# Retention attention and two feed-forward layers in one kernel: the state summed in PSUM with scaled tables, and a written order for everything up to the fourteenth product

## The chip, the cores and the metric

One core of one Trainium2 chip. The metric is the device time of one execution of the whole program in microseconds, the median of three runs; beside it stands one execution taken by the hardware profiler, whose span runs from its first to its last instruction.

## The reference

Attention with a decaying state over 2 batches of 8 heads, 768 positions and 64 features, then two feed-forward layers over the 1536 tokens of 512 features, all in float32:

```python
for t in range(S):
    state = gamma[None, :, None, None] * state + np.einsum('bhd,bhe->bhde', k[:, :, t], v[:, :, t])
    y[:, :, t] = scale * np.einsum('bhd,bhde->bhe', q[:, :, t], state)
...
rms = np.sqrt(np.mean(x * x, axis=-1, keepdims=True) + 1e-06)
xn = x / rms * rms_g
g = xn @ w_gate
silu = g * (1.0 / (1.0 + np.exp(-g)))
x = silu * (xn @ w_val) @ w_out          # d_ff 1536
...
h = x @ w_in                             # d_ff 2048
out = np.maximum(0.01 * h, h) @ w_out
```

`gamma` has one value for each head, the same at every position. The weights come as float64 bits and are converted on the chip.

## The kernel before

**Attention.** The 1536 tokens are 12 chunks of 128, six for each batch. A chunk holds 4 pairs of heads; a pair's two heads lie on partitions 0 to 63 and 64 to 127. For a chunk c the steps are, by the names of the functions: `scores` (eight matmuls on halves of the rows, k against q, into one of two score buffers), `decay_scores` (DVE multiplies by the mask of decays, tile `a`), `decay_k` (k by a table over the positions, tile `kd`; on DVE for chunks 0 and 1, on POOL from 2), `outer` (kd against v for a pair of heads at once, so that a 128 by 128 product `u` is made of which the two 64 by 64 blocks on the diagonal are used), `decay_state` (POOL: the old state by its decay, `tmp`), `update` (DVE: the two blocks of `u` plus `tmp`, one instruction for each half of the partitions, into one of two `state` tiles), `decay_q` (POOL, `qs`), `before` (the state against qs into `y`), `heads` (v against `a`, added into the same `y`), `squares` (ScalarE: y squared, and y times the gain in four instructions, `xg`), and `sums_of_squares` (DVE, one reduction). y alternates between two PSUM banks.

Two chunks together are then normalised: `total` (PE sums over the partitions), `mean` (DVE), `rsqrt` (POOL), `spread` (PE, back over the partitions), `scaled` (DVE: xg times it), `high` (ScalarE) and `rest` (DVE), which split x into a high and a low part, `xh` and `xl`, for three blocks of 512 tokens.

**Weights.** Each block of 512 KB is fetched by SyncE's queue into one of three raw buffers and converted: `prepare` (two ScalarE instructions), `smaller`, `shifted`, `sign`, `add` (DVE), `high_part` (ScalarE), `low_part` (DVE). For most weights sums and differences of two are made too (keys with an s).

**Layers.** A product (`whole`, L460) is twelve matmuls of 128 by 128 by 512: eight with the high part of x and four with the low. `gated`, `times` and `leaky` take it out of PSUM; `down` adds into four banks (L488). `quad` makes the products of two features with two blocks in seven half products (L662). `plan` lists all steps; `run` does one and lets `convert` do a number of weight steps behind it.

**Order.** Every engine works through its queue in the order in which the instructions were issued. In the attention the loop over the chunks is written out (lines 816 to 867): the tail of one chunk stands among the next chunk's steps, the total of a pair three chunks after its first. The loads of chunks 0 to 4 are issued ahead of the loop, the others four chunks ahead in it; some weight steps stand behind each chunk (`CONVERT`). The last pairs' norms are put between the first products (`late`). The first fourteen steps of the plan are the twelve products of features 0 and 1 with three blocks and two `down`:

```python
for i, (keys, b, step) in enumerate(steps[:FIXED]):
    for do in late.get(i, []):
        do()
    run(i, keys, b, step, RATE0)
```

Of the kernel before, what the change touches and what calls it, by code (L numbers as in the profile page):

```python
# [37 lines left out]
BLOCKS = [512, 512, 512]  # L38


@with_exitstack
def chain_kernel(ctx: ExitStack, tc: tile.TileContext, qk_t, kv, w1, w2, mask, qdec, kdec, sdec, rms_g, ident, out):
# [24 lines left out]
    at = attn_pools.enter_context(tc.tile_pool(name="at", bufs=2))  # L67
    at1 = attn_pools.enter_context(tc.tile_pool(name="at1", bufs=1))
# [4 lines left out]
    kdec_sb = const.tile([P, 2 * NPAIR, 1], F32, name="kdec_sb")  # L73
    sdec_sb = const.tile([P, NPAIR, 1], F32, name="sdec_sb")
# [4 lines left out]
    state = [const.tile([P, NPAIR, P], F32, name=f"state{i}") for i in range(2)]  # L79
# [18 lines left out]
    def load_chunk(c):  # L98
        if c < EARLY:
            a, b = (units.tile([P, 2, 512], F32, tag="u", name=f"{n}{c}") for n in ("qkT", "kv"))  # L100
        elif c < EARLY + len(SPARE):
            t = xp.tile([P, 4, 512], F32, tag=SPARE[c - EARLY], name=f"qkv{c}")
            a, b = t[:, :2], t[:, 2:]
        else:
            a, b = (at.tile([P, 2, 512], F32, tag=n, name=f"{n}{c}") for n in ("qkT", "kv"))
        nc.sync.dma_start(out=a, in_=qk_t[c])
        ch[c] = {"qkT": a, "kv": b}
        if c == 1:
            nc.sync.dma_start(out=qdec_sb, in_=qdec)
        if 2 < c < 6:  # L110
            fetch()
        nc.sync.dma_start(out=b, in_=kv[c])
        if c == 0:
            for j in range(2):
                nc.sync.dma_start(out=mask_sb[:, j], in_=mask[:, j])
# [9 lines left out]
    def decay_k(c):  # L125
        if not last(c):
            s = ch[c]
            s["kd"] = at1.tile([P, 2 * NPAIR, D], F32, tag="kd", name=f"kd{c}")
            e = nc.vector if c < 2 else nc.gpsimd
            e.tensor_tensor(  # L130
                out=s["kd"],
                in0=s["kv"][:, 0, :].rearrange("p (h d) -> p h d", d=D),
                in1=kdec_sb.to_broadcast([P, 2 * NPAIR, D]),
                op=ALU.mult,
            )

    def decay_q(c):
        if c % CPB:
            s = ch[c]
            s["qs"] = at1.tile([P, NPAIR, CH], F32, tag="qs", name=f"qs{c}")  # L140
            nc.gpsimd.tensor_tensor(out=s["qs"], in0=by_pair(s["qkT"][:, 0, :]), in1=qdec_sb, op=ALU.mult)

    def decay_state(c):
        if c % CPB and not last(c):
            s = ch[c]
            s["tmp"] = by_pair(scratch(f"tmp{c}"))
            nc.gpsimd.tensor_tensor(
                out=s["tmp"], in0=state[(c + 1) % 2], in1=sdec_sb.to_broadcast([P, NPAIR, P]), op=ALU.mult
            )
# [16 lines left out]

    def outer(c):
        if not last(c):
            s = ch[c]
            s["u"] = u = acc_bank(2, f"u{c}")  # L170
            kd = s["kd"].rearrange("p h d -> p (h d)")
# [4 lines left out]
    def update(c, j):  # L176
        if not last(c):
            s = ch[c]
            r = slice(j * D, (j + 1) * D)
            new, u = state[c % 2][r, :, r], by_pair(s["u"])[r, :, r]  # L180
            if c % CPB:
                nc.vector.tensor_tensor(out=new, in0=u, in1=s["tmp"][r, :, r], op=ALU.add)
            else:
                nc.vector.tensor_copy(new, u)

    def before(c):
        s = ch[c]
        s["y"] = y = acc_bank(c % 2, f"y{c}")
        for a in range(NPAIR if c % CPB else 0):
            nc.tensor.matmul(  # L190
                out=y[:, a * CH:(a + 1) * CH],
                lhsT=state[(c + 1) % 2][:, a, :],
                rhs=s["qs"][:, a, :],
                start=(a == 0),
                stop=False,
                skip_group_check=True,
            )

    def heads(c):
        s = ch[c]  # L200
        for a in range(NPAIR):
# [11 lines left out]
    def squares(c):  # L213
        s = ch[c]
        b = block_of(c)
        y = s["y"]
        s["sq"] = sq = scratch(f"sq{c}")
        nc.scalar.activation(out=sq, in_=y, func=AF.Square)
# [3 lines left out]
        for a in range(NPAIR):  # L222
            nc.scalar.activation(
                out=xg[b][:, a, o:o + CH], in_=y[:, a * CH:(a + 1) * CH], func=AF.Copy, scale=g_sb[:, a, :]
            )

    def sums_of_squares(c):
        s = ch[c]
        s["ss"] = sm.tile([P, CH], F32, tag="ss", name=f"ss{c}")
        nc.vector.tensor_reduce(out=s["ss"], in_=s["sq"].rearrange("p (a t) -> p t a", a=NPAIR), op=ALU.add, axis=AX.X)  # L230

    def total(cs):
        nrm[cs] = {"bank": acc_bank(3, f"norm{cs[0]}")}
        for i, c in enumerate(cs):
            o = 2 * CH + i
            nc.tensor.matmul(out=nrm[cs]["bank"][:, o:o + 1], lhsT=ch.pop(c)["ss"], rhs=ones, start=True, stop=True)

    def mean(cs):
# [4 lines left out]
        nc.vector.tensor_scalar(w["a"], w["bank"][:, 2 * CH:2 * CH + n], 1.0 / DM, EPS, ALU.mult, ALU.add)  # L243
# [5 lines left out]
    def spread(cs):  # L249
        w = nrm[cs]  # L250
        for i in range(len(cs)):
            nc.tensor.matmul(
                out=w["bank"][:, i * CH:(i + 1) * CH],
                lhsT=w["r"][:, i:i + 1].to_broadcast([P, P]),
                rhs=ident_sb,
                start=True,
                stop=True,
            )
# [6 lines left out]
    def scaled(cs):  # L265
        b, o = span(cs)
        if b not in xh:
            xh[b] = xp.tile([P, NPAIR, BLOCKS[b]], F32R, tag=f"xh{b}", name=f"xh{b}")
            xl[b] = xp.tile([P, NPAIR, BLOCKS[b]], F32R, tag=f"xl{b}", name=f"xl{b}")
# [4 lines left out]
    def high(cs):  # L274
        b, o = span(cs)
        own = slice(0, NPAIR)
        nc.scalar.activation(out=xh[b][:, own, o], in_=xg[b][:, own, o], func=AF.Copy)

    def rest(cs):
        b, o = span(cs)  # L280
        own = slice(0, NPAIR)
        nc.vector.tensor_tensor(
# [41 lines left out]
    def start_unit():  # L324
        if started[0] == len(wq):
            return False
# [10 lines left out]
        if src is None:  # L337
# [4 lines left out]
            if None in places:  # L342
                free(*names)
                return False
# [11 lines left out]
            def low_part(u, x, k):  # L356
# [6 lines left out]
            converting.extend(tails)  # L363
            converting.extend([
                combine(e[:, two], e[:, one], e[:, two], ALU.add),
                combine(e[:, one], a[:, one], e[:, one], ALU.subtract),
                combine(a[:, one], e[:, two], a[:, one], ALU.subtract),
                high_part(us[1], e),
                combine(a[:, two], a[:, two], a[:, one], ALU.subtract),
                high_part(us[0], a),  # L370
            ])
            tails[:] = [low_part(us[1], e, names[1]), low_part(us[0], a, names[0])]
            return True
        slot = room(key)
        if slot is None:
            return False
# [33 lines left out]
        if key not in prepared:  # L410
# [569 lines left out]
```

## Time and profile before

| what | value |
|---|---|
| median of three runs | 606.46 us (604.91 to 606.78) |
| the profiled execution | 605.0 us, span 603.2 us |
| mean granted TensorE clock | 0.993 |
| PE, DVE, ScalarE, POOL busy | 589.8, 455.5, 324.0, 37.9 us |
| instructions | 7810 |
| HBM read and written | 49.09 and 3.15 MB |

The attention runs to about 66 us of the span and the layers from there to its end. Lines such as L174 are lines of the kernel. An engine's busy time says how long it held instructions, not that something waited for it.

### The profile page before, as it was taken

The numbers are of one execution on the slowest core, as the hardware profiler recorded it, in microseconds if no ns is written. First come the engines' busy times: TensorE is split into PE (matmuls) and PEld (weight loads), VectorE is DVE, ScalarE is ACT, GpSimd is POOL, SyncE is SP. The second block draws the span as 40 slices with busy tenths as digits, with TensorE's granted clock in tenths as the row PEclk, the third lists the DMA queues.
The fourth block names the chain that finished last, engine by engine and source line by source line (L and its number), as shares of the span: only waits on it lengthen the run. The fifth ranks groups of instructions, "written<-read, shape, count | busy, mean of one in ns | idle before, by whom it ended". The sixth has DMA issues, their size and how long they took to land.

```text
span 603.2 us, 7810 instructions
## 1 busy us (share of the span) xinstructions
PE 589.8 (98%) x2939; PEld 488.8 (81%) x2939; DVE 455.5 (76%) x776; ACT 324.0 (54%) x572; POOL 37.9 (6%) x38
## 2 busy tenths in 40 slices
PE   6988999999999999999999999999999999999997
PEld 4877888888888888888888888888888888888885
DVE  4898999999888589588688988876857884631243
ACT  1554654776765465455464665877745574323320
POOL 3648100000000000000000000000000000000000
PEclk9988999999999999999999999999999999999999
DMA  8982112333522312213321130422402210000013
GB/s 334 355 335 81 46 61 69 108 106 103 174 71 75 100 35 71 70 36 104 105 70 36 39 102 0 140 70 71 139 2 70 71 35 1 0 1 1 0 70 139
DMA packets 16020, 52.73 MB, mean 87 GB/s; under 512 B 2160, under 2 KB 2288, under 8 KB 15984
## 3 DMA queue, kind: packets, MB, share of 16 engines
q1 hardware_dynamic: 15408, 52.17, 25.9%
q8 instruction: 23, 0.38, 0.3%
q10 hardware_dynamic: 576, 0.07, 0.1%
q14 instruction: 13, 0.11, 0.1%
HBM read 49.09 MB, written 3.15 MB: 87 GB/s over the span
## 4 chain that ended last, share of the span: by engine, by line
PE 93%; DVE 3%; DMA 2%; issue 1%; POOL 1%; ACT 0%; ACTq 0%; DVEq 0%
PE ap L488 21%; PE ao L488 16%; PE v L460 7%; PE g L460 7%; PE iX L662 7%; PE i L460 7%; PE vX L662 5%; PE gX L662 5%; PE iZ L662 4%; PE gZ L662 2%; PE vZ L662 2%; PE iY L662 2%; PE y L204 1%; PE y L190 1%; PE vY L662 1%; PE gY L662 1%
## 5 line engine op out<-in xcount | busy, mean ns | idle before, releaser
L488 PE MATMUL ap<-w_p,gp_2h 128*128 128x512 f32 x128 | 39.4, 389 | 0.0
L488 PE MATMUL ap<-w_p,gp_0h 128*128 128x512 f32 x128 | 39.4, 389 | 0.0
L488 PE MATMUL ap<-w_p,gp_1h 128*128 128x512 f32 x128 | 39.4, 389 | 0.0
L503 DVE TENSOR_TENSOR gp_0l<-i,gp_0h 128x512 fp32r<-128x512 f32 x16 | 11.0, 690 | 34.7 <-ACT gp_0h L496 34.7
L460 PE MATMUL g<-xh,w_g 128*128 128x512 f32 x128 | 32.2, 391 | 0.0
L460 PE MATMUL v<-xh,w_v 128*128 128x512 f32 x128 | 31.8, 391 | 0.0
L460 PE MATMUL i<-x2h,w_i 128*128 128x512 f32 x128 | 31.6, 389 | 0.0
L488 PE MATMUL ao<-go_0h,w_o 128*128 128x512 f32 x96 | 31.5, 389 | 0.0
L488 PE MATMUL ao<-go_2h,w_o 128*128 128x512 f32 x96 | 31.5, 389 | 0.0
L565 DVE TENSOR_TENSOR y2acc<-ap,y2acc 128x512 f32<-128x512 f32 x36 | 23.3, 687 | 10.4 <-PE ap L488 10.4
L488 PE MATMUL ao<-go_1h,w_o 128*128 128x512 f32 x96 | 30.5, 389 | 0.0
L488 PEld LDWEIGHTS ap<-w_p,gp_0h 128*128 128x128 f32 x128 | 24.0, 188 | 5.0
L488 PEld LDWEIGHTS ap<-w_p,gp_1h 128*128 128x128 f32 x128 | 24.0, 188 | 5.0
L488 PEld LDWEIGHTS ap<-w_p,gp_2h 128*128 128x128 f32 x128 | 24.0, 188 | 5.0
L460 PEld LDWEIGHTS i<-x2h,w_i 128*128 128x128 f32 x128 | 24.0, 188 | 5.0
L460 PEld LDWEIGHTS g<-xh,w_g 128*128 128x128 f32 x128 | 23.9, 188 | 4.9
L460 PEld LDWEIGHTS v<-xh,w_v 128*128 128x128 f32 x128 | 23.9, 188 | 4.9
L488 PE MATMUL ap<-w_p,gp_0l 128*128 128x512 f32 x64 | 24.9, 389 | 0.0
L488 PE MATMUL ap<-w_p,gp_1l 128*128 128x512 f32 x64 | 24.9, 389 | 0.0
L488 PE MATMUL ap<-w_p,gp_2l 128*128 128x512 f32 x64 | 24.9, 389 | 0.0
L503 DVE TENSOR_TENSOR gp_2l<-hold,gp_2h 128x512 fp32r<-128x512 f32 x16 | 11.0, 689 | 16.4 <-ACT gp_2h L496 12.4
L488 PEld LDWEIGHTS ao<-go_0h,w_o 128*128 128x128 f32 x96 | 18.0, 188 | 3.7
(240 smaller groups left out, 1590.5 us busy)
## 6 DMA issues: line engine op xcount, KB each, us to landing
raw_i<-in_w SPq DMA_DIRECT2D x16, 512.0 KB, 3.6
raw_p<-in_w SPq DMA_DIRECT2D x16, 512.0 KB, 3.7
raw_g<-in_w SPq DMA_DIRECT2D x12, 512.0 KB, 3.7
raw_v<-in_w SPq DMA_DIRECT2D x12, 512.0 KB, 3.6
raw_o<-in_w SPq DMA_DIRECT2D x12, 512.0 KB, 3.7
qkT<-in_qk_t SPq DMA_DIRECT2D x7, 512.0 KB, 6.6
kv<-in_kv SPq DMA_DIRECT2D x7, 512.0 KB, 8.2
out<-y2acc SPq DMA_DIRECT2D x12, 256.0 KB, 2.1
```

The costliest lines, as they stand in the source:

```text
L190: nc.tensor.matmul(out=y[:, a * CH:(a + 1) * CH], lhsT=state[(c + 1) % 2][:, a, :], rhs=s["qs"][:, a, :], start=(a == 0), stop=False, skip ...
L204: nc.tensor.matmul(out=s["y"][j * D:(j + 1) * D, a * CH:(a + 1) * CH], lhsT=s["kv"][:, 1, e:e + D], rhs=s["a"][:, j, a, :], start=not c % CPB,
L460: nc.tensor.matmul(out=dst, lhsT=lhs, rhs=rhs, start=(n == 0), stop=(n == len(pairs) - 1))
L488: nc.tensor.matmul(out=acc["b"][m], lhsT=lhs, rhs=rhs, start=(start and n == 0), stop=(stop and n == 2))
L503: nc.vector.tensor_tensor(out=l, in0=x, in1=h.bitcast(F32), op=ALU.subtract)
L565: nc.vector.tensor_tensor(out=dst, in0=banks[m], in1=dst, op=ALU.add)
L662: nc.tensor.matmul(out=dst, lhsT=lhs, rhs=rhs, start=(start and n == 0), stop=(n == 5), skip_group_check=True)
```

## The change

The decays move into tables. The key table of chunk i of a batch is divided by the head's decay over i chunks (`tables_k`: one reciprocal and four products of eight values a partition), so that the outer products of a batch are summed in one PSUM bank, in the matmuls' own accumulation; reading the state out multiplies it by the decay over the chunks (`tables_s`). `outer` makes only the 64 by 64 blocks that are used, in eight matmuls; the state is 128 by 4 by 64, `before` works on its 64 by 64 blocks, `update` is one instruction, `decay_state` is gone, and so is the zeroing of the states. `decay_k` runs on DVE for five chunks (`KD`) and on ScalarE, one head at a time, for the other five. The reduction of the squares becomes two additions; `total` and `spread` write half the partitions at a time.

All loads but chunk 11's are issued at the start in the order of `LOADS` (q and k stand for a chunk's two loads, m the mask, d the decay table of q, w a weight). A string, `ORDER`, writes out every step up to the fourteenth product: mostly two chunks are worked side by side. Tokens are step and chunk or pair of chunks, `g0:3` is the third weight step of g0, M and N are the first eight and the last four matmuls of a product, C its way out of PSUM, D a `down`, U and L its high and low part, T the sums of x for the half products. The fourteen steps keep their order among the layers' steps; behind them the plan goes on as before.

```diff
+LOADS = "q0 k0 m q1 k1 q2 d k2 k3 q3 q4 q5 k4 w w q6 q7 k6 w k8 k7 k5 q8 q9 k9 q10 k10"
-RATE0 = 4.0
-CONVERT = [0, 0, 3, 4, 3, 3, 2, 2, 2, 2, 2, 2]
+KD = (0, 3, 4, 6, 7)
+ORDER = """
+sc0 kd0 ts tk ou0 ds0 up0 sc1 kd1 he0 load ds1 sq0 ou1 qs1 xg0 sc2 up1 fa0 kd2 yi1 qs2 ds2 kd3 he1 sa0 qs3 ou2 sq1 sc3
+up2 xg1 fa1 qs4 ou3 ds3 sc4 up3 sc5 sa1 kd4 yi2 ds5 g0:P yi3 qs5 ds4 g1:P ou4 he2 g0:1 up4 g0:2 he3 g1:1 sq2 g0:3 xg2
+sc6 fa2 g1:2 sa2 sc7 g0:4 sq3 kd6 xg3 yi4 ds7 v0:P yi5 qs7 ds6 ou6 kd8 to0 v0:1 up6 he4 kd7 g0:H me0 fa3 ou7 rs0 sq4
+g0:L he5 xg4 fa4 sa3 up7 v0:2 sq5 sc8 sa4 v0:3 xg5 qs8 sc9 ds8 yi7 qs9 ds9 kd9 ou8 fa5 to1 v0:4 sp0 qs10 up8 v0:H he6
+me1 xs0 kd10 ou9 rs1 he7 sa5 up9 sq6 g1:3 sc10 sq7 v0:L xg6 fa6 sc11 fa7 sa6 sa7 xg7 ds11 yi8 hi0 yi9 g1:4 ds10 qs11
+g1:H ou10 he8 v1:P up10 lo0 he9 sq8 sp1 g1:L sq9 to3 fa8 xg8 to2 v1:1 xs1 xg9 yi10 me2 v1:2 rs2 hi1 fa9 yi11 v1:3 sa9
+o0:P me3 v1:4 he10 rs3 lo1 he11 o1:P o0:1 sp2 sa8 sq10 o0:2 layers Mg00 xs2 sq11 xg10 fa11 fa10 Ng00 sa11 xg11 sa10
+o1:1 Mg10 o0:3 hi2 o1:2 o0:4 v1:H lo2 Ng10 o0:H g2:P v1:L sp3 o0:L to5 to4 Cg10 xs3 Cg00 Mv00 me5 o1:3 hi3 rs5 me4
+o1:4 rs4 Nv00 lo3 o1:H g3:P Mv10 o1:L g2:1 Cv00 Nv10 g2:2 Uo00 g3:1 g2:3 sp4 Lo00 Mg01 xs4 Cv10 hi4 Ng01 g2:4 Uo10
...
-    state = [const.tile([P, NPAIR, P], F32, name=f"state{i}") for i in range(2)]
+    state = [const.tile([P, NPAIR, D], F32, name=f"state{i}") for i in range(4)]
...
-            e = nc.vector if c < 2 else nc.gpsimd
-            e.tensor_tensor(
...
+            if c in KD:
+                nc.vector.tensor_tensor(
...
+            for h in range(2 * NPAIR):
+                nc.scalar.activation(
+                    out=s["kd"][:, h, :], in_=s["kv"][:, 0, h * D:(h + 1) * D], func=AF.Copy, scale=kdecs[:, c % CPB, h, :]
+                )
...
-    def decay_state(c):
...
     def outer(c):
...
-                t = slice(a * P, (a + 1) * P)
-                nc.tensor.matmul(out=u[:, t], lhsT=kd[:, t], rhs=s["kv"][:, 1, t], start=True, stop=True)
...
+                for j in range(2):
+                    e = a * P + j * D
+                    nc.tensor.matmul(
+                        out=u[j * D:(j + 1) * D, a * D:(a + 1) * D],
+                        lhsT=s["kd"][:, 2 * a + j, :],
+                        rhs=s["kv"][:, 1, e:e + D],
+                        start=(i == 0 and a == 0),
+                        stop=True,
+                        skip_group_check=True,
+                    )
...
-            if c % CPB:
-                nc.vector.tensor_tensor(out=new, in0=u, in1=s["tmp"][r, :, r], op=ALU.add)
-            else:
-                nc.vector.tensor_copy(new, u)
...
+        if i == 0:
+            nc.vector.tensor_copy(new, u)
+        else:
+            nc.vector.tensor_tensor(out=new, in0=u, in1=sdecs[:, i - 1].to_broadcast([P, NPAIR, D]), op=ALU.mult)
...
+            for j in range(2):
+                r = slice(j * D, (j + 1) * D)
+                nc.tensor.matmul(
+                    out=y[r, a * CH:(a + 1) * CH],
+                    lhsT=state[(c - 1) % 4][r, a, :],
+                    rhs=s["qs"][r, a, :],
...
-        nc.vector.tensor_reduce(out=s["ss"], in_=s["sq"].rearrange("p (a t) -> p t a", a=NPAIR), op=ALU.add, axis=AX.X)
+        nc.vector.tensor_tensor(out=half, in0=half, in1=s["sq"][:, 2 * CH:], op=ALU.add)
...
+        nc.vector.tensor_tensor(out=s["ss"], in0=s["sq"][:, :CH], in1=s["sq"][:, CH:2 * CH], op=ALU.add)
...
+                nc.tensor.matmul(out=nrm[cs]["bank"][r, o:o + 1], lhsT=ss[:, r], rhs=ones, start=True, stop=True)
...
+                nc.tensor.matmul(
+                    out=w["bank"][j * D:(j + 1) * D, i * CH:(i + 1) * CH],
+                    lhsT=w["r"][:, i:i + 1].to_broadcast([P, D]),
...
+    load(*LOADS.split())
...
+        for token in ORDER.split():
+            do(token)
```

## Rows read from the trace of the kernel before

**Rows 1.** The page's table of engines: busy us (share of the span), instructions.

```profile
PE 589.8 (98%) x2939; PEld 488.8 (81%) x2939; DVE 455.5 (76%) x776; ACT 324.0 (54%) x572; POOL 37.9 (6%) x38
```

**Rows 2.** The chain that ended last, in order of time: start us, us, what.

```profile
78.96 5.44 PE g L460 x24
...
597.05 2.73 DVE y2acc L565 x4
```

**Rows 3.** Windows: length; busy PE, PEld, DVE, ACT, POOL; clock, DMA share, GB/s.

```profile
4.27:14.54 10.27, 6.81 (x72) 5.80 (x72) 6.32 (x9) 1.63 (x5) 3.00 (x3) 1.00 1.01 387
14.54:66.29 51.75, 47.20 (x509) 42.09 (x509) 47.34 (x65) 26.82 (x67) 31.99 (x28) 0.93 0.61 229
66.29:78.80 12.51, 12.51 (x63) 10.37 (x62) 11.38 (x19) 8.44 (x16) 1.76 (x2) 1.00 0.29 85
78.80:106.16 27.36, 27.36 (x122) 22.68 (x121) 26.28 (x39) 14.22 (x23) 0.00 (x0) 1.00 0.21 60
106.16:166.00 59.84, 59.84 (x265) 49.30 (x264) 57.62 (x112) 44.09 (x79) 0.00 (x0) 1.00 0.40 123
```

**Rows 4.** Who waited for whom, 4 to 66.3 us: us, times, longest.

```profile
PE norm L236 <- DVE ss L230: 4.1, 3, 1.7
...
DVE a L165 <- PE sc L159: 3.5, 2, 2.1
...
PE y L190 <- POOL qs L141: 0.4, 1, 0.4
```

**Rows 5.** Timeline of PE: start us, us, line, out<-in, weights, moving operand [idle before].

```profile
46.06 1.16 PE L159 MATMUL sc<-qkv 64*128 64x128 f32 x16
47.16 1.16 PE L174 MATMUL u<-qkv,kd 128*128 128x128 f32 x8
48.15 0.61 PE L252 MATMUL norm<-ident_sb,nr 128*128 128x128 f32 x4
48.60 1.10 PE L190 MATMUL y<-qs,state 128*128 128x128 f32 x8
49.63 1.09 PE L204 MATMUL y<-a,qkv 128*64 128x128 f32 x16
50.65 1.16 PE L159 MATMUL sc<-qkT 64*128 64x128 f32 x16
...
54.72 0.38 PE L236 MATMUL norm<-ones,ss 128*128 128x1 f32 x2 [1.70 <-DVE ss L230]
54.96 1.91 PE L190 MATMUL y<-qs,state 128*128 128x128 f32 x8
56.79 1.93 PE L204 MATMUL y<-a,qkv 128*64 128x128 f32 x16
...
65.82 0.61 PE L236 MATMUL norm<-ones,ss 128*128 128x1 f32 x4
66.29 2.08 PE L460 MATMUL g<-xh,w_g 128*128 128x512 f32 x8
```

**Rows 6.** Groups on DVE, 0 to 80 us: busy us, mean ns | idle.

```profile
L230 DVE TENSOR_REDUCE ss<-sq 128x128 f32<-128x512 f32 x12 | 12.6, 1051 | 0.0
L272 DVE TENSOR_TENSOR xg<-xg,norm 128x1024 f32<-128x1024 f32 x6 | 7.3, 1219 | 0.1
L182 DVE TENSOR_TENSOR state<-u,tmp 64x256 f32<-64x256 f32 x16 | 6.7, 419 | 0.3
...
L130 DVE TENSOR_TENSOR kd<-kv,kdec_sb 128x512 f32<-128x512 f32 x2 | 2.3, 1131 | 6.5 <-DMA kv<-in_kv 6.5
...
L391 DVE SCALAR_TENSOR_TENSOR wa_g<-raw_g,wa_g 128x512 int32<-128x512 int32 x2 | 1.4, 687 | 0.0
```

**Rows 7.** Groups of instructions on ScalarE, 0 to 80 us.

```profile
L223 ACT ACTIVATE xg<-y,g_sb 128x128 f32<-128x128 f32 x48 | 13.7, 376 | 0.0
L218 ACT ACTIVATE sq<-y 128x512 f32<-128x512 f32 x12 | 7.1, 592 | 16.8 <-PE y L204 14.5 <-POOL kd L130 2.3
```

**Rows 8.** A window of the loads: columns as in rows 3.

```profile
10.00:20.00 10.00, 7.95 (x98) 7.25 (x98) 6.86 (x7) 3.89 (x12) 6.36 (x7) 1.00 1.02 408
```

More of the change, by code (lines that the diff above doesn't have):

```diff
@@ L139, in decay_q @@
             s = ch[c]
-            s["qs"] = at1.tile([P, NPAIR, CH], F32, tag="qs", name=f"qs{c}")
+            s["qs"] = gp.tile([P, NPAIR, CH], F32, tag="gl", name=f"qs{c}")
             nc.gpsimd.tensor_tensor(out=s["qs"], in0=by_pair(s["qkT"][:, 0, :]), in1=qdec_sb, op=ALU.mult)
-    def decay_state(c):
[L144 to L149, printed above, removed]
     def scores(c):
@@ L189, in before @@
         for a in range(NPAIR if c % CPB else 0):
[L190 to L197, printed above, removed]
+            for j in range(2):
+                r = slice(j * D, (j + 1) * D)
[3 more added lines that the diff above has]
+                    rhs=s["qs"][r, a, :],
+                    start=(a == 0),
+                    stop=False,
+                    skip_group_check=True,
+                )
     def heads(c):
         s = ch[c]
+        if not c % CPB:
+            before(c)
         for a in range(NPAIR):
@@ L343, in start_unit @@
                 free(*names)
-                return False
+                return None
             started[0] += 1
@@ L813, in pair, with tables_k @@
-    def pair(c):
-        return (c, c + 1) if 0 <= c < NCHUNK and c % 2 == 0 else None
+    load(*LOADS.split())
+    def pair(p):
+        return 2 * p, 2 * p + 1
+    def tables_k():
+        nc.vector.reciprocal(out=turn, in_=turn)
+        for i in range(1, CPB - 1):
+            nc.vector.tensor_tensor(
+                out=kdecs[:, i, :, 0].rearrange("p (a j) -> p j a", j=2),
+                in0=kdecs[:, i - 1, :, 0].rearrange("p (a j) -> p j a", j=2),
+                in1=turn,
+                op=ALU.mult,
+            )
@@ new lines, in layers @@
+    def layers():
+        score_pool.close()
+        pools["ps"] = ctx.enter_context(tc.tile_pool(name="ps", bufs=4, space=bass.MemoryType.PSUM))
+    by_chunk = {
+        "sc": scores, "ds": decay_scores, "yi": before, "ou": outer, "up": update, "kd": decay_k, "qs": decay_q,
+        "he": heads, "sq": squares, "xg": gains, "fa": first_sum, "sa": second_sum,
+    }
+    by_pair_of = {"to": total, "me": mean, "rs": rsqrt, "sp": spread, "xs": scaled, "hi": high, "lo": rest}
+    alone = {
+        "open": reopen, "layers": layers, "load": lambda: load("q11", "k11"), "tk": tables_k, "ts": tables_s
+    }
@@ L904, in chain_kernel, with run @@
-        for i, (keys, b, step) in enumerate(steps[:FIXED]):
-            for do in late.get(i, []):
-                do()
-            run(i, keys, b, step, RATE0)
+        for token in ORDER.split():
+            do(token)
+        for unit in opened_units.values():
+            if unit[2]:
+                queue(unit)
+        sums.extend(in_pairs(terms))
+    owed = 0.0
+    def run(i, keys, b, step, rate):
+        nonlocal owed
+        need(keys[0])
+        step()
+        next_parts(upper)
+        for _ in range(min(len(sums), SUMS)):
+            sums.pop(0)()
+        owed += rate * (0.5 if keys[-1] == "half" else 1.0)
+        convert(int(owed))
+        owed -= int(owed)
+        next_parts(lower)
```

366 lines of the change are left out of this document (186 added, 180 removed).

## The prediction

> **What bounds the kernel now.** I read the page's engine table first: PE is busy for 98% of the span [rows 1]. A busy share is an average over two stages, so the next view is the chain that ended last. From the first products on it is nearly all PE: products at 2.72 us for twelve matmuls, without a wait, up to the last ones; after them come 2.73 us of DVE and the last output [rows 2]. The windows agree: from 66.29 to 166 us PE is busy in every microsecond and the granted clock is 1.00 [rows 3]. So whatever lets PE start the layers earlier moves the end by the same amount, if nothing later starves PE, and the change is worth what it takes out of the attention stage before 66.29 us.
>
> What is lost there? I price the attention's matmuls at full speed from the starts of consecutive groups [rows 5]: scores 1.10 us a chunk (46.06 to 47.16), outer products 0.99, state into y 1.03, the heads' products 1.02, one pair's spread 0.45, one pair's total 0.47 (65.82 to 66.29). With 12, 10, 10, 12, 4 and 5 of them this is 13.20 + 9.90 + 10.30 + 12.24 + 1.80 + 2.35 = 49.8 us, and PE spent 66.29 - 4.27 = 62.0 us on them: 12.2 us are lost. The first stretch, 4.27 to 14.54 us, holds 6.2 us of this work in 10.3 us, so 4.0 us are lost there, and the second holds 43.6 in 51.75, so 8.2 us. The waits name 4.1 us for sums of squares that DVE makes late and 0.4 us for a decayed q [rows 4]; the reader is to see that PE waits there for work which no product needs yet, because the total stands ahead of them in PE's queue. The rest is mostly the clock: it is 0.93 of full over the second stretch [rows 3], and behind the wait that ends at 54.72 us the state product runs 1.91 us in place of 1.10 and the heads' 1.93 in place of 1.09 [rows 5], the 1.2 GHz level. That spell costs 1.65 us; 0.07 of 51.75 us is 3.6, so there is room for two of them. DVE is busy for 47.3 of these 51.75 us, ScalarE for 26.8, POOL for 32.0 [rows 3]. So PE waits, DVE is nearly full, and each reads the other's results.
>
> **The change part by part.** *DVE.* The state's update becomes one instruction on 128 partitions in place of two on 64, with the same 256 elements each: 20 times 0.42 us becomes 10 times 0.42, 4.2 us less [rows 6]. The reduction at 1.05 us becomes two additions of 256 and 128 elements. The first is as long as the update, 0.42; the second lies between that and nothing, and I take 0.29. So 12 times 1.05 becomes 12 times 0.71, 4.1 us less. DVE decays k for five chunks in place of two, 3 times 1.13 = 3.4 us more. Eight tiny table operations, each well under 0.42 us, fall into the first stretch, where DVE waits for data anyway; if that cover were gone they would delay the first masked scores by 1 to 2 us. Balance: 4.9 us less. What the order asks of DVE ahead of the first product differs a little too: four weight steps more (two at 0.69 us, two that I take at 0.42), two scalings of x at 1.22 and one chunk's sum less, 0.9 us less in all [rows 6]. So DVE needs 47.3 - 4.9 - 0.9 = 41.5 us.
>
> *PE.* The outer product goes from four matmuls of 128 by 128 by 128 to eight of 128 by 64 by 64 in sixteen records. No row shows this shape. The nearest, the heads' (128 by 64, 128 columns), runs sixteen records in 1.02 us [rows 5]; with half the columns it could be 0.51. I take 0.85, near the upper end, since the weight loads stay sixteen: nine later ones save 1.3 us (bounds: 0.3 more to 4.3 less). The state product goes to sixteen records of 64 by 64, 128 columns; its neighbours on both sides, scores and heads, take 1.10 and 1.02, so I leave it at 1.03. Total and spread double their records at half the width: nothing to 0.9 us for a pair, I take 0.5 us for all. The first stretch takes in one more scores (order: sc2 ahead of yi1), 1.1 us out of idle time. One total and one spread move behind the first product: they are not saved.
>
> *ScalarE* decays k for five chunks with eight instructions of 64 elements. The nearest row is the gain's, 128 elements, 13.7 us for 48, 0.285 each [rows 7]; I take that as the upper bound and 0.2 as the lower, 8 to 11.4 us in all. With 26.8 busy of 51.75 us this is hidden. Without that cover, two chunks in a row whose y banks it must free would hold PE.
>
> *POOL* loses eight decayed states and eight decayed k; its queue keeps ten decayed q and the reciprocal roots, and in the trace PE waited 0.4 us for it [rows 4]. Worth that.
>
> *SP.* All loads are issued first, in a new order; each weight after the third now queues behind chunk 11. At 408 GB/s [rows 8] the 24 chunk loads, mask, decay table and three weights, 14.9 MB, take 36.6 us. Before, the decay table was the fifth item (2.36 MB, 5.8 us at that rate) and the second chunk's decayed q came in time for the heads at 14.54 us; now 3.41 MB go up to the table, 2.6 us more. What slack there was goes with it, so I expect those heads at about 14.5 us, as before, and the first stretch gains only the 1.1 us. Chunk 11 waits for the buffers of chunk 0, which are free within the first stretch, and only weights stand behind it. Chunk 5's k and v, the 21st half megabyte, comes by about 31.5 us, where a dense PE wants it at 33; the rest is earlier than needed. Cost nothing; if the rate fell by a tenth, about 2 us.
>
> *The stalls.* Dense PE gains 8.2 + 1.1 + 1.3 - 0.5 = 10.1 us. Not all of it can come: PE's own work from 14.54 us to the first product is then 43.6 - 1.1 - 1.3 - 0.9 + 0.3 = 40.6 us, and DVE's 41.5. Two queues in strict order, both nearly full, wait for each other. I keep 3 us of waits: 0.5 at the y banks (square 0.59 and gains 1.14 us of one chunk before its bank comes back), 2.5 at DVE. What is late next is the scaled x of the later blocks: between the first product and the end of the fourteenth PE has 39.9 us and DVE was busy for 37.7 of them [rows 3]; the order adds about 3 us of weight steps there, but those at the end are used first 20 us later, so I charge nothing.
>
> Sum: 10.1 - 3.0 = 7.1 us. The profiled execution took 605.0 us with a span of 603.2, so it would take 597.9; it stands 1.5 us under the median of the runs, which gives 606.5 - 7.1 = 599.4 us.
>
> **A rule that speaks against it.** The state product's two halves of rows now write two halves of the partitions of one bank; in the scores each half of rows had a bank of its own. Heads with halves of columns in one bank run at 64 ns a record [rows 5], but no row shows halves of rows in one. The Trainium skill, TensorEngine Tiling, section Gotcha 1: PSUM Pressure, says that different row tiles cannot access the same bank at one time. By the row the ten products cost 10.3 us; by the rule they would take turns, as in the first rival.
>
> **Rivals.** (a) *The halves take turns.* Sixteen records at the 128-wide rate, 1.03/8 = 0.129 us, are 2.06 us a chunk, 1.03 us more, 10.3 us over ten. It would swallow the waits that I kept, so the gain lies between 10.1 - 10.3 and 7.1 - 10.3: 606.5 to 609.7 us. For it: nothing in the trace; against it: halves of columns share a bank at full rate. (b) *DVE sets the pace.* If it idles as it did, 4.4 us of the stretch, the stretch takes 41.5 + 4.4 = 45.9 us, the first product starts at 60.4 and, less 0.9 for the norm moved behind it, 5.0 us are gained; with 1 to 2 us more lost at the later blocks, 602 to 603.5 us. For it: DVE is busy at 91% now. Against: 3.5 us of its idle time were two waits for late scores [rows 4], which now come earlier. (c) *Slower: the clock.* The wait of 1.7 us [rows 4] that ended at 54.72 us was followed by a spell at the low level in which the work ran 1.75 times as long [rows 5]. If the new order breaks PE's work into short runs, the level could stay low: at 0.75 us lost for each us of work, the 7.1 us of gain are gone with 9.5 us of such work (two full chunks have 8.3), and a third of the 43.6 us at that level costs 10.9 and gives 606.5 - 7.1 + 10.9 = 610.3 us. Against it: the order puts scores and outer products of a later pair between dependent steps. (d) *Given back.* PE comes 7 us earlier to the weights of group two while DVE was busy for 57.6 of 59.8 us from 106 to 166 us [rows 3]. If a weight were late by that much, the time would stay at 606. Against it: PE had not one wait there. (e) *All of it.* No new waits and outer products at 0.51: 10.1 + 3.1 = 13.2 us, 593.3; with outer products as taken, 596.4.
>
> **How the numbers follow.** Forecast 0.56 (596.5 to 601.5), (b) 0.16, (e) 0.10, (a) 0.08, (c) 0.06, (d) 0.04. The forecast, (b) up to its end and most of (e) make the range: 594.5 to 604.0 us. No change, within 0.3% (1.8 us, about what a measurement of this kernel can tell), takes (d), half of (a) and the tail of (b), 0.10; slower takes (c) and the rest of (a), 0.08; faster 0.82.
>
> **What would show it.** Right: the first g product starts near 58 us, PE's waits for the sums of squares are gone, the clock of the second stretch is above 0.97, eight outer matmuls take 0.8 to 0.9 us, the products stay at 2.72 us to the end. Wrong: state products of 2 us (a); PE waiting for DVE's scaled or rest parts of block one and two (b); a clock under 0.9 (c); PE waits after 100 us (d).

## The result and the profile after

The changed kernel takes 598.13 us (597.88 to 598.30, four runs) against 606.6 us of the kernel before on the same chip: ratio 0.9866, 95% interval 0.9848 to 0.9884. The forecast was 599.4 us in a range of 594.5 to 604.0; its 597.9 us for a profiled execution stands against 598.3. The sum came out right, but the start and the stretch behind it were off by about 4 us each, in opposite directions. The profiled span fell by 6.7 us (603.2 to 596.5), the median by 8.5: the profiled execution before was one of its faster ones, while the changed kernel's four runs lie within 0.4 us.

The page's engine table of the changed kernel, to be read against [rows 1]: PE works 6.4 us less, DVE 9.7 us less, POOL 17 us less, ScalarE 10 us more.

```profile
PE 583.4 (98%) x3147; PEld 482.5 (81%) x3147; DVE 445.8 (75%) x789; ACT 334.2 (56%) x612; POOL 20.7 (3%) x20
```

Windows of the changed kernel, columns as in [rows 3]. The first product starts at 57.91 us in place of 66.29.

```profile
4.27:14.54 10.27, 6.37 (x65) 5.73 (x66) 4.63 (x13) 2.34 (x6) 0.34 (x1) 0.79 0.98 345
10.50:17.00 6.50, 6.05 (x58) 5.74 (x60) 2.12 (x3) 4.80 (x15) 2.50 (x2) 0.50 1.00 405
18.00:40.00 22.00, 20.55 (x382) 18.60 (x380) 21.83 (x37) 16.44 (x52) 10.24 (x7) 1.00 1.03 408
40.00:57.91 17.91, 15.24 (x287) 13.74 (x283) 17.71 (x34) 15.21 (x41) 5.91 (x6) 1.00 0.39 130
14.54:57.91 43.37, 39.26 (x701) 35.56 (x697) 40.76 (x72) 35.10 (x105) 18.35 (x14) 0.97 0.76 294
57.91:66.00 8.09, 8.09 (x56) 6.60 (x55) 7.97 (x16) 7.99 (x18) 0.00 (x0) 1.00 0.26 83
...
```

Three things are to be seen. The first window is worse than before: the granted clock is 0.79 there and the loads run at 345 GB/s, where it was 1.00 and 387. From 10.5 to 17 us the clock is 0.50, the 1.2 GHz level. From 18 us on DVE is busy for 39.54 of 39.91 us, so it has 0.4 us to spare, while PE idles for 4.1. And from 57.91 to 100 us PE has no gap, as before; behind 100 us it waits once, for 0.2 us.

PE's waits in the attention, 4 to 58 us (us, times, longest), against [rows 4]:

```profile
PE sc L175 <- DMA qkT<-in_qk_t: 3.5, 1, 3.5
PE u L195 <- DVE kd L149: 1.6, 2, 1.2
PE u L195 <- issue: 1.0, 1, 1.0
PE y L220 <- ACT xg L256: 0.9, 1, 0.9
...
```

The waits for sums of squares are gone, as the order meant. The largest is new: the second chunk's scores wait 3.5 us for their q. PE's timeline before, for the second chunk's scores and heads:

```profile
9.38 1.16 PE L159 MATMUL sc<-qkT 64*128 64x128 f32 x16
...
14.54 1.09 PE L204 MATMUL y<-a,kv 128*64 128x128 f32 x16
```

The same timeline in the changed kernel shows what followed the wait, and, against [rows 5], what the new operations cost:

```profile
6.79 0.68 PE L195 MATMUL u<-kv,kd 128*64 128x64 f32 x16 [0.42 <-DVE kd L149]
10.95 2.08 PE L175 MATMUL sc<-qkT 64*128 64x128 f32 x16 [3.48 <-DMA qkT<-in_qk_t]
12.96 1.98 PE L236 MATMUL y<-a,kv 128*64 128x128 f32 x16
...
15.97 1.66 PE L175 MATMUL sc<-qkT 64*128 64x128 f32 x16
17.55 1.09 PE L220 MATMUL y<-qs,state 64*64 64x128 f32 x16
18.57 1.09 PE L236 MATMUL y<-a,kv 128*64 128x128 f32 x16
...
28.32 2.06 PE L175 MATMUL sc<-qkv 64*128 64x128 f32 x32
30.30 1.96 PE L220 MATMUL y<-qs,state 64*64 64x128 f32 x32
32.19 0.69 PE L195 MATMUL u<-qkv,kd 128*64 128x64 f32 x16
32.71 0.35 PE L279 MATMUL norm<-ones,ss 128*64 128x1 f32 x8
...
57.91 2.11 PE L526 MATMUL g<-xh,w_g 128*128 128x512 f32 x8
```

After the wait scores take 2.01 us (10.95 to 12.96) where the second chunk took 1.16 before, and the second chunk's heads stand at 18.57 us where they stood at 14.54: 4.0 us are lost at the start. (The scores at 15.97 us are the third chunk's, which the new order puts ahead of these heads, 1.1 us at full speed.) By the starts, sixteen records of the outer product take 0.52 us (32.19 to 32.71) and of the state product 1.02 (17.55 to 18.57).

The new groups on DVE and ScalarE, 0 to 80 us, against [rows 6] and [rows 7] (two views, DVE first):

```profile
L263 DVE TENSOR_TENSOR sq<-sq 128x256 f32<-128x256 f32 x12 | 5.1, 429 | 0.0
L268 DVE TENSOR_TENSOR ss<-sq 128x128 f32<-128x128 f32 x12 | 4.3, 369 | 0.0
L212 DVE TENSOR_TENSOR state<-u,sdecs 128x256 f32<-128x256 f32 x8 | 3.3, 413 | 2.0 <-PE u L195 2.0
L149 DVE TENSOR_TENSOR kd<-qkv,kdecs 128x512 f32<-128x512 f32 x2 | 1.3, 674 | 0.0
```

```profile
L157 ACT ACTIVATE kd<-kv,kdecs 128x64 f32<-128x64 f32 x24 | 6.0, 340 | 0.0
L157 ACT ACTIVATE kd<-qkv,kdecs 128x64 f32<-128x64 f32 x16 | 4.1, 367 | 0.0
```

The start of ScalarE changed too. Its table load, 1.28 us, was done early before; now its first work is the second chunk's decayed k, and the table load stands with it behind that chunk's load (ScalarE's timeline, before and then changed):

```profile
2.62 1.28 ACT L218 ACT_TABLE_LOAD   x1 [2.62 <-issue]
```

```profile
12.19 1.28 ACT L157 ACT_TABLE_LOAD   x1 [12.19 <-DMA kv<-in_kv]
```

### The profile page after: what moved, and what is told of

Its sections match the earlier page's. It is cut to its first block, busy times and chain, and to the rows that moved or that the text cites. A ratio compares the mean times of both kernels' runs of the same rounds, so it can differ in the third digit from the quotient of the medians.

```text
span 596.5 us, 8244 instructions
## 1 busy us (share of the span) xinstructions
PE 583.4 (98%) x3147; PEld 482.5 (81%) x3147; DVE 445.8 (75%) x789; ACT 334.2 (56%) x612; POOL 20.7 (3%) x20
## 4 chain that ended last, share of the span: by engine, by line
PE 93%; DVE 4%; DMA 2%; issue 1%; ACT 1%; ACTq 0%
PE ap L556 21%; PE ao L556 16%; PE g L526 7%; PE v L526 7%; PE i L526 7%; PE iX L753 7%; PE gX L753 5%; PE vX L753 5%; PE iZ L753 4%; PE gZ L753 2%; PE vZ L753 2%; PE iY L753 2%; PE sc L175 2%; PE y L236 1%; PE vY L753 1%; PE gY L753 1%
## 5 line engine op out<-in xcount | busy, mean ns | idle before, releaser
L564 ACT ACTIVATE gp_2h<-hold 128x512 fp32r<-128x512 f32 x16 | 10.1, 631 | 20.2 <-PE ap L556 20.2
```

Source lines behind the costliest of these rows:

```text
L564: nc.scalar.activation(out=h, in_=x, func=AF.Copy)
```

## The experiments

Each ratio below is against the kernel before, run beside it on the same chip. All runs after the result fall into three groups: what the operations and the order are worth, what the start lost, and what sets the pace from 18 us on.

**The changed kernel again**, unedited, as a control.

> The changed kernel once more, as a control on the same chip as the three beside it: 598.1 us, within 0.5. In its trace the first chunk's scores ran 2.08 us (1.16 in the kernel before) and PE stood 3.5 us ahead of the second chunk's. If the wait comes from the order of the loads it is there again, 3.3 to 3.7 us; if it was one execution's accident it is not.

598.92 us (598.41 to 599.83), ratio 0.9887 (0.987 to 0.9904): 0.3 us more than the expected spread allowed. PE's wait for the second q was there again (3.7 us); the second chunk's scores started at 11.09 us, its heads at 18.17 and the first product at 58.01. From those heads to the first product it took 39.8 us, 39.3 in the first profile.

**The outer products twice**, the second copy into unused columns.

```diff
+                    for again in range(2):
+                        f = a * D + again * NPAIR * D
-                        out=u[j * D:(j + 1) * D, a * D:(a + 1) * D],
+                            out=us[-1][j * D:(j + 1) * D, f:f + D],
```

> Every outer product is made twice, the second time into the unused half of its bank (its result is used by nothing). That is 0.51 us more PE work for each of ten chunks, 5.1 us. Theory A, PE sets the end and the smaller outer product is worth its full time: 3 to 5 us more (part of it falls into PE's remaining waits of 4 us), 601 to 603 us. Rival B, DVE sets the pace and PE's savings are hidden: under 1 us more, below 599 us.

600.86 us (600.57 to 601.86), ratio 0.992 (0.9905 to 0.9935): 2 us more than the control, between the numbers of the two theories. Its second chunk's heads stood at 20.32 us (18.57 in the first profile), partly because its first loads came later. From there to the first product it took 41.1 us in place of 39.3 to 39.9 in the three profiles with the same order (the two above and the next run): nine outer products more, 4.2 to 4.7 us of PE's work, cost 1.1 to 1.7. Adding work to PE is mostly hidden.

**The small loads later**, behind the first six big ones.

```diff
+    load(*LOADS.split()[:6])
     nc.scalar.dma_start(out=g_sb, in_=rms_g)
     nc.scalar.dma_start(out=ident_sb, in_=ident)
-    load(*LOADS.split())
+    load(*LOADS.split()[6:])
```

> The loads of the gain and of the identity are issued behind the first six items of the load list in place of ahead of all. In the trace the mask's load waits until the key table has landed, and the second chunk's q until a table of 2 KB has: each load seems to wait for the load eight before it. Theory A, this gate starves PE at the start: the second chunk's q is issued at about 4.4 us in place of 6.2, its scores start at 9.2 to 9.5 in place of 10.95, the clock does not fall, and 2 to 4 us are gained, 594 to 596 us. Rival B, the start is bound by the bytes themselves and the rest of the stage makes up for it anyway: under 0.5 us, 597.6 to 598.2 us.

599.4 us (598.8 to 600.32), ratio 0.989 (0.9872 to 0.9908). Neither expected number came. SyncE's queue issued the same loads in the same order as in the changed kernel, and the second q at 6.62 us (6.18 there), so this is a second control and tells nothing of the loads. It does show how far the start varies by itself: PE's wait for the second q was 4.5 us in that profile, the second chunk's heads stood at 19.88 and the first product started at 59.82.

**The new operations in the engine order of before**, loads in the old order.

```diff
-LOADS = "q0 k0 m q1 k1 q2 d k2 k3 q3 q4 q5 k4 w w q6 q7 k6 w k8 k7 k5 q8 q9 k9 q10 k10"
+LOADS = "q0 k0 m q1 d k1 q2 k2 q3 w k3 q4 w k4 q5 w k5 q6 k6 q7 k7 q8 k8 q9 k9 q10 k10"
-sc0 kd0 ts tk ou0 ds0 up0 sc1 kd1 he0 load ds1 sq0 ou1 qs1 xg0 sc2 up1 fa0 kd2 yi1 qs2 ds2 kd3 he1 sa0 qs3 ou2 sq1 sc3
...
+sc0 kd0 ts tk ds0 ou0 up0 qs1 he0 sc1 kd1 ds1 sq0 xg0 ou1 kd2 up1 yi1 qs2 he1 sq1 xg1 sc2 ds2 sc3 fa0 sa0 ds3 ou2 kd3
...
```

> All new operations (scaled tables, smaller outer products, one update, two additions, k on ScalarE), but every engine's order up to the fourteenth product as in the kernel before, and the loads in the order of before (all issued at the start). Theory A, the operations give PE 4.8 us and DVE 5 us of less work but the waits for the sums of squares and the low clock come back with the old order: 601 to 604 us. Rival B, the operations are the whole gain and the order adds nothing: 597 to 599 us. Rival C, the operations are hidden without the order: 605 us or more.

606.6 us (606.32 to 608.05), ratio 1.0017 (1.0004 to 1.0031), the number of rival C: without the order the whole change is worth nothing. PE's waits in that kernel, 4 to 67 us, are those of the kernel before, and a new one behind ScalarE's decayed k, whose table load ran from 13.41 us on:

```profile
PE norm L279 <- DVE ss L268: 3.7, 4, 1.6
PE u L195 <- ACT kd L157: 1.8, 1, 1.8
...
```

The second chunk's heads stood at 19.08 us and the first product at 66.91. From the one to the other took 47.8 us, 4 less than before (51.75) and 8.5 more than in the changed kernel (39.3). So the operations gave 4 us there, the start took about as much away, and the order gave the rest. (Of the 8.5, about 2 are work that the order moves to either side of this stretch: one chunk's scores and one pair's norm.) No run has the new order with the old operations, so what the order would give without them is not known.

**The mask as one load, gain and identity on SyncE's queue**, so that the second q is among the first eight loads. In the changed kernel SyncE's queue itself waits between 0 and 12 us for small loads of ScalarE's queue, and the second q is issued at 6.18 us (4.41 before):

```profile
SPq L122 <- DMA kdecs<-in_kdec: 2.7, 1, 2.7
SPq L132 <- DMA turn<-in_sdec: 1.1, 1, 1.1
```

```diff
-                for j in range(2):
-                    nc.sync.dma_start(out=mask_sb[:, j], in_=mask[:, j])
+                nc.sync.dma_start(out=mask_sb, in_=mask)
...
-    nc.scalar.dma_start(out=g_sb, in_=rms_g)
-    nc.scalar.dma_start(out=ident_sb, in_=ident)
-    load(*LOADS.split())
+    load(*LOADS.split()[:6])
+    nc.sync.dma_start(out=g_sb, in_=rms_g)
+    load(*LOADS.split()[6:12])
+    nc.sync.dma_start(out=ident_sb, in_=ident)
+    load(*LOADS.split()[12:])
```

> The changed kernel, but the gain and identity tables are fetched by SyncE's queue behind the first loads and the mask is one load in place of two, so that the second chunk's q is among the first eight loads of the program. Theory (each load waits for the one issued eight before it; two more small loads made the second chunk's q late, PE then waits about 3.5 us and its granted clock drops to 0.50 from 10.5 to 17 us): SyncE issues the second chunk's q without a wait, its scores start at 7.5 to 9.5 us in place of 10.95, the clock between 4.27 and 14.54 us is 1.00 again, the first product starts 2 to 4 us earlier (54 to 56 us), and the time is 594 to 596.7 us. Rival (the first stretch is limited by the rate of the loads, not by when they are issued): first product within 1 us of 57.9, time 598 to 599.5 us. Second rival (an earlier start only meets later data, and DVE): starts earlier but the gain is given back before the first product, 597 to 599 us.

598.54 us (598.08 to 598.89), ratio 0.9877 (0.9853 to 0.9901): no gain, a number that both rivals gave. The second q was issued at 2.11 us, and its scores still started at 10.21, behind another wait for it (1.6 us). The first product came at 57.27 us, 0.6 earlier, and up to 113.9 us PE then waited 0.4 us for ScalarE, which it did not in the changed kernel. DVE's timeline shows a second cost: the 2 KB table of the state's decays came at 10.27 us, and everything behind it on DVE waited.

```profile
7.15 0.69 DVE L148 TENSOR_TENSOR kd<-kv,kdecs 128x512 f32<-128x512 f32 x1 [6.00 <-DMA kv<-in_kv]
10.27 0.56 DVE L919 TENSOR_TENSOR sdecs<-sdecs 128x4 f32<-128x4 f32 x3 [2.43 <-DMA sdecs<-in_sdec]
```

So an early issue alone does not bring the second q early. The same edit in the old order:

> The new operations in the engine order of the kernel before, with the same edit of the loads as in the run with the early gate. That order with the loads as changed took 606.6 us. Theory (the late second chunk cost it about 4 us): the second chunk's heads come at 14 to 15.5 us in place of 19.08, first product 62 to 64 us, 602 to 604 us. Rival (the start is not what held it): 605.5 us or more.

607.28 us (606.46 to 608.91), ratio 1.003 (1.0014 to 1.0046); second heads at 19.16 us, first product at 66.73. The theory's number missed here too, but the run hardly tests it: PE stood 4.9 us, to 13.50, behind DVE's masked scores of the first chunk, and DVE behind the same 2 KB table (10.42 us).

**The two 2 KB loads alone, in the kernel before.**

```diff
+    turn = const.tile([P, 2, NPAIR], F32, name="turn")
...
+    for j in range(2):
+        nc.scalar.dma_start(out=turn[:, j], in_=sdec[j * D:j * D + 1, :, 0].to_broadcast([P, NPAIR]))
```

> The kernel before, with two loads of 2 KB more on ScalarE's queue, the ones that the change adds; nothing reads them. Theory (they take two of the first eight places, so the mask and the second chunk's q wait for other loads): the second chunk's scores start 1.5 us or more later than 9.38 us, the clock of 4.27 to 14.54 us falls, and the time is 1.5 to 4.5 us over the kernel before. Rival (2 KB cost nothing): within 1 us of it.

608.77 us (606.75 to 610.07), ratio 1.0046 (1.0028 to 1.0064): 4 KB that nothing reads cost 2.8 us by the ratio (1.7 to 3.9), 3.3 between the medians. PE's timeline, against [rows 5] and 9.38 us for these scores before; the clock of 14.54 to 20 us was 0.50:

```profile
11.23 1.16 PE L160 MATMUL sc<-qkT 64*128 64x128 f32 x16 [1.03 <-DMA qkT<-in_qk_t]
15.46 0.77 PE L175 MATMUL u<-kv,kd 128*128 128x128 f32 x2 [3.06 <-DVE kd L131]
```

**The changed kernel without these two loads**: PE makes the eight values from the table that is loaded anyway (`pick` is zero but for one row of ones).

```diff
-    for j in range(2):
-        nc.scalar.dma_start(out=turn[:, j], in_=sdec[j * D:j * D + 1, :, 0].to_broadcast([P, NPAIR]))
+    def turns():
+        nrm["bank"] = acc_bank(3, "norm")
+        for j in range(2):
+            o = 3 * CH + j * NPAIR
+            nc.tensor.matmul(out=nrm["bank"][:, o:o + NPAIR], lhsT=pick[:, j], rhs=sdecs[:, 0, :, 0], start=True, stop=True)
-sc0 kd0 ts tk
+sc0 tu kd0 ts tk
```

> The changed kernel without its two extra 2 KB loads: the eight decays that they brought to every partition are made from the table of the state's decays that is loaded anyway, by two matmuls against a tile with a single row of ones; the first eight loads are again those of the kernel before. Theory (those two loads, and not when the later ones are issued, delay everything behind them: in the run with the early gate the second chunk's q was issued at 2.11 us and still came at about 10.2 us): the second chunk's scores start at 9.0 to 9.8 us in place of 10.95, the mean clock of 4.27 to 14.54 us is over 0.9, the first product starts at 54.5 to 57 us, the time is 595.5 to 598 us. Rival (DVE is the pace from 18 us on, idle for 1.1 us of 40, so that an earlier start of PE is given back): the earlier scores are there, but the first product within 0.7 us of 57.9 and the time 598 to 599.5 us.

596.9 us (596.41 to 597.17), ratio 0.9857 (0.9842 to 0.9873), the theory's number. PE's timeline and a window:

```profile
9.13 1.16 PE L176 MATMUL sc<-qkT 64*128 64x128 f32 x16 [1.81 <-DMA qkT<-in_qk_t]
...
12.09 2.00 PE L196 MATMUL u<-kv,kd 128*64 128x64 f32 x16 [0.78 <-ACT kd L158]
...
16.13 1.09 PE L237 MATMUL y<-a,kv 128*64 128x128 f32 x16
...
56.83 2.11 PE L527 MATMUL g<-xh,w_g 128*128 128x512 f32 x8
```

```profile
4.27:14.54 10.27, 7.08 (x93) 5.95 (x94) 5.04 (x15) 4.13 (x12) 2.15 (x2) 1.00 1.02 391
```

The clock is 1.00 again and the loads run at 391 GB/s. The second heads come 2.4 us earlier, the first product only 1.1: the rest is given back on the way. Those heads are still 1.6 us later than before, and the line at 12.09 us shows a second loss: ScalarE's table load held it from 10.40 to 11.68 us, its eight activations took 2.02 us behind that, and PE's outer products, after a wait of 0.78 us, ran at their pace (1.93 us in place of 0.52). No run takes the table load forward, so what that is worth is not known. 1.1 us is also what the loads gained in the first window, (391 - 345) GB/s for 10.27 us or 0.47 MB, which take 1.15 us at 408 GB/s.

**Three moves in the order**, on top of the edit of the mask: chunk 8's update ahead of the weight step `v0:4` on DVE, chunk 6's gain ahead of chunk 10's decayed k on ScalarE, chunk 8's gain ahead of chunk 9's squares.

```diff
-... fa5 to1 v0:4 sp0 qs10 up8 v0:H he6
+... fa5 to1 up8 v0:4 sp0 qs10 v0:H he6
-... kd10 ou9 rs1 he7 sa5 up9 sq6 g1:3 sc10 sq7 v0:L xg6 ...
+... ou9 rs1 he7 sa5 up9 sq6 g1:3 sc10 xg6 sq7 v0:L kd10 ...
-... sq9 to3 fa8 xg8 to2 ...
+... xg8 to3 fa8 sq9 to2 ...
```

> The run with the early gate, and three moves in the written order: the update of chunk 8 ahead of a weight step on DVE, the gain of chunk 6 ahead of the decayed k of chunk 10 on ScalarE, the gain of chunk 8 ahead of the squares of chunk 9. Theory (the three waits of 1.0, 0.73 and 0.94 us that PE had left at 42.9, 47.2 and 53.5 us are each behind one late instruction of DVE or ScalarE): the three waits fall to under 0.3 us each, the time is 1 to 2.5 us under that of the early gate alone. Rival (what PE does not wait for here it waits for at the next DVE result, since DVE is busy for 38.9 of 41.5 us): the same time within 0.8 us, and a wait of the same length at another place.

598.57 us (597.74 to 599.36), ratio 0.9878 (0.9856 to 0.9901), and 598.54 without the moves: the rival. PE's waits between 18 and 58 us changed their places and not their sum (4.2 us here and 4.2 without the moves):

```profile
PE y L219 <- POOL qs L164: 2.0, 1, 2.0
PE u L194 <- DVE kd L148: 1.2, 1, 1.2
PE sc L174 <- DVE a L180: 0.5, 1, 0.5
PE y L219 <- issue: 0.5, 1, 0.5
```

**More work for DVE**: the old reduction in place of the two additions.

```diff
-        nc.vector.tensor_tensor(out=half, in0=half, in1=s["sq"][:, 2 * CH:], op=ALU.add)
+        nc.vector.tensor_reduce(out=s["ss"], in_=s["sq"].rearrange("p (a t) -> p t a", a=NPAIR), op=ALU.add, axis=AX.X)
...
-        nc.vector.tensor_tensor(out=s["ss"], in0=s["sq"][:, :CH], in1=s["sq"][:, CH:2 * CH], op=ALU.add)
```

> The changed kernel with the reduction of the kernel before (one instruction, 1.05 us) in place of the two additions, at the place of the first. The additions took 0.41 and 0.27 us, so DVE has 0.37 us more for each of the nine to ten chunks summed ahead of the first product: 3.5 us. Theory (DVE sets the pace): the first product 2.5 to 3.7 us later, 600.9 to 602.5 us. Rival: PE's waits cover it, under 1 us later, 598.3 to 599.9 us.

603.14 us (601.89 to 604.29), ratio 0.9961 (0.9945 to 0.9976): 4 us above the controls, 0.6 above the theory's range. The second heads stood at 18.52 us as before the edit, the first product at 61.85, 3.9 us later. That is all of DVE's 3.5 us and a little more, but not by DVE alone: PE's wait of 1.57 us was followed by work at the low clock.

```profile
55.80 2.89 PE L220 MATMUL y<-qs,state 64*64 64x128 f32 x32 [1.57 <-ACT xg L256]
```

By the starts, the state products and heads of two chunks took 5.5 us there and 3.9 in the changed kernel, and the granted clock from 55.80 us to the first product was 0.72. So 1.6 of the 3.9 us are the clock, and some 2.3 are DVE's 3.5 met directly. The windows, which end at the same time as those of the changed kernel:

```profile
18.00:40.00 22.00, 20.47 (x372) 18.39 (x368) 21.19 (x30) 16.40 (x51) 8.78 (x7) 1.00 1.03 408
40.00:57.91 17.91, 13.23 (x246) 12.06 (x246) 17.82 (x25) 12.87 (x40) 3.47 (x4) 0.98 0.34 119
```

DVE is full, and PE has 2.0 us less done in the second.

**Less work for DVE**: the decayed k of chunks 3, 4, 6 and 7 on POOL.

```diff
-                nc.vector.tensor_tensor(
+                (nc.vector if c == 0 else nc.gpsimd).tensor_tensor(
```

> The changed kernel with the decayed k of chunks 3, 4, 6 and 7 on POOL in place of DVE (1.04 us each there in the kernel before); the start is as in the changed kernel. Theory (DVE sets the pace from 18 us on): DVE loses 4 times about 1.1 us, the first product starts 2.5 to 4.5 us earlier, at 53.5 to 55.5 us, and the time is 594 to 596.5 us. Rival (PE, with the waits of two strict queues, sets it): DVE gets idle time, the first product moves by under 1 us, 597.5 to 599.5 us.

599.27 us (598.76 to 600.28), ratio 0.9901 (0.9885 to 0.9918), first product at 58.23 us: no gain, against the theory. Its windows, and POOL's waits between 18 and 58 us:

```profile
18.00:40.00 22.00, 20.96 (x390) 18.94 (x388) 19.23 (x32) 17.14 (x53) 12.07 (x11) 1.00 1.03 410
40.00:57.91 17.91, 14.75 (x276) 13.43 (x274) 17.74 (x34) 15.30 (x43) 5.24 (x5) 1.00 0.42 143
```

```profile
POOL kd L149 <- DMA qkv<-in_kv: 5.1, 2, 3.5
POOL kd L149 <- DMA kv<-in_kv: 2.2, 1, 2.2
```

DVE idles for 2.9 us, nearly all of it before 40 us, and what it could do earlier is not ready: three of the four decayed k wait for their chunk's load to land. Behind 40 us, where no decayed k was moved, DVE is as full as before.

**Both**, no small loads and four decayed k on POOL.

> The run without the two loads and the run with four decayed k on POOL together. Theory (the start and DVE are two separate losses, and the first is worth something only where DVE has room): the gains add up or more, first product at 52 to 54.5 us, 592.5 to 595.5 us. Rival (PE's other waits or POOL's queue take over): no better than the better one of the two by over 0.6 us.

596.8 us (596.71 to 597.27), ratio 0.9858 (0.9843 to 0.9873): the rival, no better than without the small loads alone. The first product did come earlier, at 56.26 us, 0.6 ahead of that run, though the clock was 0.50 from 10 to 15 us again; but PE then waited 0.5 us for ScalarE up to 112.9 us, a wait that the other run lacks. So an earlier first product is no longer worth its full amount here. These two are the fastest versions that were run; against the changed kernel's 0.9866, 0.9887 and 0.989 the gain is 0.1 to 0.3%, at the edge of what the intervals tell.

## Why the prediction was right, step by step

**What held.** PE bounds, and what it saves before the layers moves the end. The first product came 8.4 us earlier (forecast: near 58 us, 57.91 measured); up to the end of the fourteenth product the doubled total and spread records and a pair's norm that was moved there took 1.4 of it back (forecast 0.9); 0.7 more went in the later layers, 0.2 of it in the one wait, and the end behind the last matmuls was 0.4 shorter. So the span is 6.7 us shorter (forecast 7.1). The waits for sums of squares went, the products of the later layers stay at 2.72 us, and of the waits of rival (d) only those 0.2 us came; in two runs with an earlier first product, 0.4 to 0.5 us did. DVE was busy for 40.76 us between 14.54 us and the first product, forecast 41.5.

**A step that failed: the loads "cost nothing".** I expected the second chunk's heads at about 14.5 us as before; they came at 18.57. I had weighed the new order of the big loads and not the two 2 KB ones that the tables need. The kernel before with these two loads alone is 2.8 us slower, the changed kernel without them starts its second heads 2.4 us earlier at full clock. That the small loads cost 2.4 of the 4.0 us is thereby shown. How 4 KB do it is not: the late issue of the second q was my theory, and the run that issued it at 2.11 us refuted it as the whole cause. The rate of the loads was lower by 11% in the first window alone, so my remark on a rate lower by a tenth throughout is not tested. For the other 1.6 us the term that most likely failed is ScalarE's, "this is hidden": in the first stretch the second chunk's decayed k stood behind the table load, and PE waited for it and then ran at its pace. That is read from the trace without the small loads; no run removes it.

**A term that was mis-sized: the outer product.** I took 0.85 us near the upper bound; it is 0.52, the lower (0.51). Over nine chunks that is 3.0 us. Scores, state and heads of two chunks in a row also take a little less than single ones in [rows 5] (1.98, 1.89 and 1.86 us for two), by my estimate from these rows together 2 to 3 us over the stretch. PE's work from the second heads to the first product is therefore 39.34 - 4.11 = 35.2 us, where I had 40.6, and the waits are 4.1 us where I kept 3. The stretch takes 39.3 in place of 43.6, and this 4.3 cancels the 4.0 lost at the start. That the two are of one size is partly luck. Partly they hang together: without the small loads the start came 2.4 us earlier and the stretch grew to 40.7 us.

**What sets the pace is not PE alone.** I added PE's work and a sum of waits. The runs say it differently: 4.2 to 4.7 us more for PE cost 1.1 to 1.7, 3.5 us more for DVE cost 3.9, with 1.6 of it the clock, waits that are moved come back elsewhere, and up to about 36 us the loads probably hold what DVE would do next. That is nearer to rival (b), which assumed 4.4 us of DVE's idle time where 2.6 were measured from 14.54 us on. (14.54 + 40.76 + 2.61 = 57.91 is only the sum of a window and no evidence.) The pace is not shown to be DVE's alone: 2.5 us less work for it gained nothing. That loads pace the first half rests on POOL's waits in two kernels and on the fact that PE's start without the small loads moved just as the loads did; no run made the loads themselves faster there.

**The rule and rival (a).** The Trainium skill, TensorEngine Tiling, section Gotcha 1: PSUM Pressure, says that different row tiles cannot use one bank at one time; by that a chunk would cost 2.06 us, an estimate from the 128-wide rate in [rows 5]. The trace differs: 1.02 us for one chunk, 1.89 for two in a row, with the two halves of rows writing different halves of the bank's partitions. Rival (a) falls by this row. (By its own sum its range began at 606.7 us, not 606.5.)

**The clock, rival (c).** It came, but at the start only: 0.50 from 10.5 to 17 us after the wait of 3.48 us. From 18 us to the first product it was 1.00, forecast above 0.97; the run with more work for DVE shows that a wait of 1.57 us there can bring it back.

## What to carry to other kernels

Cost the small loads too: where PE's start waits for the first big transfers, 4 KB in small pieces (288 packets more under 512 B on the page) took more time than any operation that they fed. Look at what an engine does first: a table load that stood free before can come to stand behind data when the first instruction changes. When two engines are both over 90% busy, ask what an added microsecond on each of them costs, not which of them waits; here it was 0.2 to 0.4 us for one on PE and about a whole one on DVE, of which the clock took over a third. New operations and a new order should be tried apart: here the operations alone gave nothing, and the order turned their slack into time.

## What the runs showed of the hardware

**DVE beside POOL.** The timeline of the changed kernel, POOL's decayed q (two in a row) and a small addition on DVE that takes 0.27 us elsewhere:

```profile
17.96 2.96 POOL L165 TENSOR_TENSOR qs<-qkT,qdec_sb 128x512 f32<-128x512 f32 x2 [1.27 <-DMA qkT<-in_qk_t]
...
19.71 1.36 DVE L268 TENSOR_TENSOR ss<-sq 128x128 f32<-128x128 f32 x1
```

It ended at 21.07 us, just after POOL's at 20.92. With four decayed k on POOL, the additions of 256 and 128 elements took 0.50 and 0.48 us in the mean up to 58 us, 0.43 and 0.39 without, so a part of what DVE handed over seems to have come back as waiting. The Trainium skill, SBUF — State Buffer, section Who interferes with whom, says that a DVE instruction with two SBUF inputs contends with a GpSimd instruction that reads SBUF. The trace agrees with it in this 1.36 us.

**Small records on PE.** Sixteen records, eight matmuls of 128 by 64 by 64 with their weights, took 32 ns a record (0.52 us). **Short activations on ScalarE.** Eight of 128 by 64 back to back took 2.02 us, 0.25 each, between my bounds of 0.2 and 0.285.

**Half speed at a granted clock of 1.00.** In the run with the small loads later, PE waited 4.51 us and then took 2.01 us for the second chunk's scores, as in the changed kernel, but the granted clock from 12 to 17 us reads 1.00 there (0.50 from 11 to 17 in the changed kernel). The cause is open; it shows that a spell is to be read from the lengths of the work as well as from the granted clock.
